# A gated mix of linear attention and an S-shifted MLP: the last 64 rows of W4 done in row tiles, and a re-ordered start

## The chip, the cores and the metric

The kernel runs on one core of one Trainium2 chip. The metric is the device time of one execution in microseconds (us); lower is better. Four runs of the kernel before took 267.59, 267.78, 267.78 and 268.14 us, the median is 267.78 us. The profile is of one further execution.

## The reference

With x of 2048 rows and 640 features, in bfloat16, the output is `g*a + (1-g)*b`, row by row:

```
g = sigmoid((x * gate_w).sum(-1))
a = linear attention of x (32 heads of 20 features, phi(q), phi(k), weights wqkv 640x1920, then wo 640x640)
h  = gelu(layernorm(x) @ w1)                       # 640 x 640
hs = (four quarters of h, shifted by +1, -1, +2, -2 rows) @ w2
x1 = x + hs
b  = x1 + gelu(layernorm(x1) @ w3) @ w4            # w3 640 x 1728, w4 1728 x 640
```

The change touches two places: the first products of the kernel, `k = x @ wk` together with the gate's dot product, and the last product, `... @ w4`, whose contraction runs over 1728 features. 1728 is 13 blocks of 128 and a rest of 64.

## The kernel before

Work is in blocks of 128 rows (16 of them, `c`), and in the MLP in tiles of 512 rows (`TS`, 4 of them, `t`), each of 4 blocks (`cc`). Every engine runs its instructions in the order in which the program writes them; nothing is rescheduled. All products go into PSUM tiles from one pool, `pair()`, of which there are four: each holds two banks of 128 x 512 float32, and a product of 640 output features is done as two halves (`hf`) of 320, one in each bank. A fifth `pair()` waits until the first is free.

**The start.** The SP queue (L124, L118, L130) and the ACT queue issue the loads: block 0 of x first, the five 128-row blocks of the k weights (`wk_sb`, one `load_wk` each; 0, 2, 4 on ACT and 1, 3 on SP), the gate vector `g5` (5 x 128) on SP, and then seven DMA transposes that bring the other blocks of x into `xT`. TensorE begins with six 512-wide products of constants (`warmup`, L202) that nobody reads, then transposes block 0 of x (L210), VectorE copies the transpose to `xT` (L211), and after two 128-wide products of constants the k products of block 0 follow (`k_mm`, L190), in the order 0, 2, 1, 4, 3 of the weight blocks and with the gate vector's transpose (L215) and its copy into column 640 of `wk_sb` (L216) in between. Blocks 1 to 15 then follow, each with ten k products of 320 or 321 columns; ScalarE and VectorE take each result out of PSUM (`k_evac`).

**The middle.** Then come q (L231), the sums over rows for the attention (L306), w1 (L340), the attention's small products (L359, L246, L378, L258), and w2 (L416). Of these, L246 and L378 use the array in narrow column tiles (the profile's form 128*32), L258 in row tiles (32*128).

**The MLP's tiles.** For each `t`, the w3 products (L463, 13 feature blocks of 128, results gelu'd by ScalarE at L471 into `h2`) alternate with the w2 products of the next tile and the attention's last product of this one (L447). The rest of 64 features of w3 (L468) is done in two column tiles (128*64), 256 rows of the tile each, so that in `h2` partitions 0 to 63 hold the 64 features for rows 0 to 255 and partitions 64 to 127 hold the same features for rows 256 to 511.

Then `w4_unit` runs for the four blocks of the tile. For each half it does 14 products of 320 columns (L488): 13 over full blocks and one over the rest. For the rest, `w4_sb` holds W4's last 64 rows twice, once in partitions 0 to 63 and once in 64 to 127, in two 128-row slots whose other half is set to zero by GpSimd (L395, L396). The product over all 128 partitions thus adds zeros for the rows of the other block. VectorE combines the result with the gate and with x1 (L494), SP stores it (L497). In the very last block each half has a `pair()` of its own and is taken out (L490) and stored (L492) by itself. `x1_scale` (L440), on ScalarE, scales the next tile's x1 by `1-g`.

Of the kernel before, what the change touches and what calls it, by code (L numbers as in the profile page):

```python
# [8 lines left out]
ALU = mybir.AluOpType  # L9
BF16 = mybir.dt.bfloat16  # L10
# [6 lines left out]
def kernel(  # L17
# [13 lines left out]
    nc = tc.nc  # L31
    P = 128
    S, D = A_x.shape[1], A_x.shape[2]
    F = B_w3.shape[1]
    H, Dh = 32, 20
    NCH = S // P
    TS = 512
    NT = S // TS
    CPT = TS // P
    DC = D // P  # L40
    HD = D // 2
    FF = F // P
    FR = F - FF * P
# [12 lines left out]
    out2 = out.rearrange("b s d -> (b s) d")  # L56
# [8 lines left out]
    outp = ctx.enter_context(tc.tile_pool(name="outp", bufs=2))  # L65
# [3 lines left out]
    def pair():  # L69
        return ps.tile([P, 2, 512], F32, name="pp")  # L70
# [15 lines left out]
    ident = const.tile([P, P], BF16)  # L86
    g5 = const.tile([DC, P], BF16)
# [8 lines left out]
    omg = const.tile([P, NCH], F32)  # L96
# [10 lines left out]
    wk_sb = st1.tile([P, DC, D + 16], BF16)  # L107
# [7 lines left out]
    sp, aq, gq = nc.sync, nc.scalar, nc.gpsimd  # L115

    def load_x(c0, c1):
        sp.dma_start(x_sb[:, c0:c1, 0:D], x2[c0 * P:c1 * P, :].rearrange("(c p) d -> p c d", p=P))  # L118
# [4 lines left out]
    def load_wk(q, dc):  # L123
        q.dma_start(wk_sb[:, dc, 0:D], A_wqkv[dc * P:(dc + 1) * P, D:2 * D])  # L124

    load_x(0, 1)
    load_wk(aq, 0)
    load_wk(aq, 2)
    load_wk(sp, 1)
    sp.dma_start(g5[:], gate_w.rearrange("(c p) -> c p", p=P))  # L130
    load_wk(aq, 4)
    load_wk(sp, 3)
    for c0, c1 in ((1, 2), (2, 3), (3, 4), (4, 6), (6, 8), (8, 12), (12, 16)):
        load_xT(c0, c1)
    sp.dma_start(wq_sb, wqkv_v[:, :, 0:D])
# [50 lines left out]
    def k_mm(pt, c, dcs, hfs=(0, 1), last=DC - 1):  # L186
        for dc in dcs:
            for hf in hfs:
                n = HD + hf
                nc.tensor.matmul(pt[:, hf, 0:n], lhsT=xT[:, dc, c * P:(c + 1) * P],  # L190
                                 rhs=wk_sb[:, dc, hf * HD:hf * HD + n], start=(dc == 0), stop=(dc == last))

    def k_evac(pt, c):
        nc.scalar.copy(ylog[:, c:c + 1], pt[:, 1, HD:HD + 1])
        phi(pk[:, c, :].rearrange("p (h e) -> p h e", h=2), pt[:, :, 0:HD], D)
# [4 lines left out]
    def warmup(n, w=TS):  # L200
        for i in range(n):
            nc.tensor.matmul(warm[:, 1, 0:w], lhsT=one[:, 0:P], rhs=one[:, 0:w], start=True, stop=True)  # L202

    warmup(6)
    kp = pair()
    turns = [(pair()[:, 0, :].bitcast(BF16), a, b) for a, b in ((0, 2), (2, DC))]
    tg = warm[:, 0, :].bitcast(BF16)
    for n, (ptb, a, b) in enumerate(turns):
        for dc in range(a, b):
            nc.tensor.transpose(ptb[:, (dc - a) * P:(dc - a + 1) * P], x_sb[:, 0, dc * P:(dc + 1) * P], ident[:])  # L210
        nc.vector.tensor_copy(xT[:, a:b, 0:P], ptb[:, 0:(b - a) * P].rearrange("p (c s) -> p c s", c=b - a))  # L211
    warmup(2, P)
    order = (0, 2, 1, 4, 3)
    k_mm(kp, 0, order[:3], (0,), order[4])
    nc.tensor.transpose(tg[:, 0:DC], g5[:], ident[0:DC, 0:DC])  # L215
    nc.vector.tensor_copy(wk_sb[:, :, D], tg[:, 0:DC])  # L216
    k_mm(kp, 0, order[3:4], (0,), order[4])
    k_mm(kp, 0, order[:4], (1,), order[4])
    k_mm(kp, 0, order[4:], last=order[4])
    k_evac(kp, 0)  # L220
    for c in range(1, NCH):
        pt = pair()
# [168 lines left out]
        ln1_apply(3 * CPT + cc)  # L391
    s1.close()
    w4p = ctx.enter_context(tc.tile_pool(name="w4p", bufs=1))
    w4_sb = w4p.tile([P, FF + 2, D], BF16)
    nc.gpsimd.memset(w4_sb[FR:P, FF, :], 0.0)  # L395
    nc.gpsimd.memset(w4_sb[0:FR, FF + 1, :], 0.0)  # L396
    nc.gpsimd.dma_start(w4_sb[:, 0:FF, :], B_w4[0:FF * P, :].rearrange("(c p) f -> p c f", p=P))
    nc.gpsimd.dma_start(w4_sb[0:FR, FF, :], B_w4[FF * P:F, :])
    nc.gpsimd.dma_start(w4_sb[FR:P, FF + 1, :], B_w4[FF * P:F, :])
    h2p = ctx.enter_context(tc.tile_pool(name="h2p", bufs=1))  # L400
    x1p = ctx.enter_context(tc.tile_pool(name="x1p", bufs=8))
    st = {}
# [6 lines left out]
    def w2_unit(t, cc):  # L409
        c = t * CPT + cc  # L410
        if cc == 0:
            st[t] = dict(x1=[], mv=small.tile([P, CPT, 2], F32, name="mv2"))
        pt = pair()
        for hf in range(2):
            for fc in range(DC):
                nc.tensor.matmul(pt[:, hf, 0:HD], lhsT=hsT[:, fc, 2 + c * P:2 + (c + 1) * P],  # L416
                                 rhs=w2_sb[:, fc, hf * HD:(hf + 1) * HD], start=(fc == 0), stop=(fc == DC - 1))
        x1 = x1p.tile([P, D], F32, name="x1")
        nc.vector.tensor_tensor(x1[:].rearrange("p (h e) -> p h e", h=2), pt[:, :, 0:HD],  # L419
                                x_sb[:, c, 0:D].rearrange("p (h e) -> p h e", h=2), op=ALU.add)  # L420
        ln_stats(st[t]["mv"][:, cc, :], x1[:], small.tile([P, 2, 6], F32, name="bnst")[:])
        st[t]["x1"].append(x1)

    def ln2_rstd(t, c0, c1):
        if c0 == 0:
            st[t]["rstd"] = small.tile([P, CPT], F32, name="rstd2")
        rsqrt(st[t]["rstd"][:, c0:c1], st[t]["mv"][:, c0:c1, 1])
# [9 lines left out]
    def x1_scale(t, cc):  # L437
        c = t * CPT + cc
        x1 = st[t]["x1"][cc]
        nc.scalar.activation(x1[:], x1[:], ACT.Copy, scale=omg[:, c:c + 1])  # L440
# [13 lines left out]
    def w3_unit(t, i):  # L454
        if "h2" not in st[t]:
            st[t]["h2"] = h2p.tile([P, FF * TS + LT], BF16, name="h2")
        h2, lnT = st[t]["h2"], st[t]["lnT"]
        pt = pair()
        for k in range(2):
            fc = 2 * i + k  # L460
            if fc < FF:
                for dc in range(DC):
                    nc.tensor.matmul(pt[:, k, :], lhsT=w3_sb[:, dc, fc * P:(fc + 1) * P], rhs=lnT[:, dc, :],  # L463
                                     start=(dc == 0), stop=(dc == DC - 1))
            else:
                for dc in range(DC):
                    for v in range(2):
                        nc.tensor.matmul(pt[FR * v:FR * (v + 1), k, 0:LT], lhsT=w3_sb[:, dc, FF * P:F],  # L468
                                         rhs=lnT[:, dc, v * LT:(v + 1) * LT], start=(dc == 0), stop=(dc == DC - 1))
        n = 2 * TS if 2 * i + 1 < FF else TS + LT  # L470
        nc.scalar.activation(h2[:, 2 * i * TS:2 * i * TS + n], pt[:].rearrange("p h e -> p (h e)")[:, 0:n],  # L471
                             ACT.Gelu_apprx_tanh)

    def w4_unit(t, cc):
        c = t * CPT + cc
        h2, x1 = st[t]["h2"], st[t]["x1"][cc]
        last = c == NCH - 1
        oc = outp.tile([P, D], BF16, name="oc")
        pts = [pair(), pair()] if last else [pair()] * 2
        for hf in range(2):  # L480
            hs = slice(hf * HD, (hf + 1) * HD)
            for fc in range(FF + 1):
                if fc < FF:
                    w, l = w4_sb[:, fc, hs], h2[:, fc * TS + cc * P:fc * TS + (cc + 1) * P]
                else:
                    v, o = cc // 2, FF * TS + (cc % 2) * P
                    w, l = w4_sb[:, FF + v, hs], h2[:, o:o + P]
                nc.tensor.matmul(pts[hf][:, hf, 0:HD], lhsT=l, rhs=w, start=(fc == 0), stop=(fc == FF))  # L488
            if last:
                nc.vector.scalar_tensor_tensor(oc[:, hs], pts[hf][:, hf, 0:HD], omg[:, c:c + 1], x1[:, hs],  # L490
                                               op0=ALU.mult, op1=ALU.add)
                nc.sync.dma_start(out2[c * P:(c + 1) * P, hs], oc[:, hs])  # L492
        if not last:
            nc.vector.scalar_tensor_tensor(oc[:].rearrange("p (h e) -> p h e", h=2), pts[0][:, :, 0:HD],  # L494
                                           omg[:, c:c + 1], x1[:].rearrange("p (h e) -> p h e", h=2),
                                           op0=ALU.mult, op1=ALU.add)
            nc.sync.dma_start(out2[c * P:(c + 1) * P, :], oc[:])  # L497

    for cc in range(CPT):
        w2_unit(0, cc)  # L500
# [16 lines left out]
    for t in range(NT):  # L517
        for i in range(NW3):
            w3_unit(t, i)
            if i < CPT and t + 1 < NT:  # L520
                w2_unit(t + 1, i)
            if 2 <= i < 2 + CPT:
                att_unit(t, i - 2)
        if t + 1 < NT:
            ln2_rstd(t + 1, 0, CPT)
            for cc in range(CPT):
                ln2_apply(t + 1, cc)
        for cc in range(CPT):
            if t + 1 < NT:
                x1_scale(t + 1, cc)  # L530
            w4_unit(t, cc)


# [28 lines left out]
```

## Time and profile before

| | |
|---|---|
| median of four runs | 267.78 us (267.59 to 268.14) |
| the profiled execution | 267.77 us |
| its span, first to last instruction | 266.1 us |
| around the span | 1.67 us |
| TensorE busy | 260.1 us, 98% of the span |
| VectorE, ScalarE, GpSimd busy | 140.3, 84.3, 24.1 us |
| DMA moved | 23.62 MB |
| chain of waits that ended last | 95% on TensorE |

Times in the profile are counted from the start of the span. A row of a group gives line, engine, operation, the tile written and those read, the form (rows*columns of the array that are used, then partitions x elements), the count, the busy time and the mean of one in ns, and behind the second bar the engine's idle time just before. "PEld" is TensorE's weight load, which has rows of its own. The durations of products overlap, since they are pipelined: what one product costs in a stream is the distance of its start from the next one's start.

### The profile page before, as it was taken

The page shows a single profiled execution, that of the slowest core. Times are in us where ns is not written, and L with a number is a line of the kernel's source. Part 1 is how long each engine was busy: PE and PEld are TensorE (multiplying, and loading weights), DVE is VectorE, ACT ScalarE, POOL GpSimd, SP SyncE. Part 2 cuts the span into 40 slices and gives each one's busy share as a digit, 9 for nine tenths or more (in the row PEclk, how much of TensorE's full clock was granted, in tenths as well). Part 3 has the DMA queues.
Part 4 walks back from the last instruction along what each step waited for, and adds up shares of the span by engine and source line. Part 5 has one row for each costly group of instructions (what it writes and reads, how often), then busy time and mean ns, then how long its engine had stood idle before and what let it go on. Part 6 is the DMA issues. An engine that isn't in the chain of part 4 may idle for free.

```text
span 266.1 us, 4240 instructions
## 1 busy us (share of the span) xinstructions
PE 260.1 (98%) x1720; PEld 163.4 (61%) x1736; DVE 140.3 (53%) x270; ACT 84.3 (32%) x122; POOL 24.1 (9%) x60
## 2 busy tenths in 40 slices
PE   7999999999999999999999999999999999999994
PEld 3677555788755644565676556577556577455673
DVE  1688688899857788945422364521464512122122
ACT  1555544321165646531510312420212340333100
POOL 7100010012323140001000001000001000000000
PEclk9999999999999999999999999999999999999999
DMA  7999977025668942000231000141000051000011
GB/s 191 174 240 365 378 229 291 0 46 122 129 96 252 201 76 52 0 0 0 46 84 48 25 0 2 25 99 52 25 0 2 1 123 52 25 0 2 0 49 49
DMA packets 44749, 23.62 MB, mean 89 GB/s; under 512 B 35450, under 2 KB 43642, under 8 KB 44730
## 3 DMA queue, kind: packets, MB, share of 16 engines
q1 hardware_dynamic: 43802, 20.57, 30.7%
q0 software_dynamic: 496, 2.29, 2.6%
q10 hardware_dynamic: 432, 0.49, 0.6%
q8 instruction: 13, 0.21, 0.3%
q14 instruction: 6, 0.05, 0.1%
HBM read 12.21 MB, written 2.62 MB: 56 GB/s over the span
## 4 chain that ended last, share of the span: by engine, by line
PE 95%; DMA 2%; ACT 1%; issue 0%; ACTq 0%; DVE 0%
PE pp L488 23%; PE pp L463 21%; PE pp L306 8%; PE pp L416 8%; PE pp L447 8%; PE pp L190 8%; PE pp L340 8%; PE pp L231 8%; DMA wk_sb<-in_A_wqkv_dram 2%; PE pp L468 1%; ACT m_sb L380 1%; PE pp L359 1%; PE pp L246 0%; ACTq L124 0%; PE pp L378 0%
## 5 line engine op out<-in xcount | busy, mean ns | idle before, releaser
L488 PE MATMUL pp<-w_sb,h 128*128 128x320 bf16 x448 | 61.5, 299 | 0.0
L471 ACT ACTIVATE h<-pp 128x1024 bf16<-128x1024 f32 (+1 forms) x28 | 27.8, 993 | 103.8 <-PE pp L463 95.4
L463 PE MATMUL pp<-lnxT,w_sb 128*128 128x512 bf16 x249 | 59.8, 379 | 0.6
L488 PEld LDWEIGHTS <-h 128*128 128x128 bf16 x448 | 43.5, 98 | 17.5 <-issue 0.8
L463 PEld LDWEIGHTS <-w_sb 128*128 128x128 bf16 x260 | 25.4, 98 | 26.7
L494 DVE SCALAR_TENSOR_TENSOR oc<-pp,omg,x 128x640 bf16<-128x640 f32 x15 | 13.3, 884 | 44.7 <-PE pp L488 44.7
L450 DVE SCALAR_TENSOR_TENSOR x<-pp,gate,x 128x640 f32<-128x640 f32 x16 | 13.9, 868 | 29.4 <-PE pp L447 29.4
L182 ACT ACTIVATE e<-pp 128x640 bf16<-128x640 f32 (+1 forms) x26 | 21.5, 827 | 9.6 <-PE pp L231 9.6
L447 PE MATMUL pp<-m_sb,pqT 128*128 128x320 bf16 x160 | 24.3, 299 | 0.0
L419 DVE TENSOR_TENSOR x<-pp,x_sb 128x640 f32<-128x640 f32 x16 | 13.1, 820 | 21.0 <-PE pp L416 21.0
L416 PE MATMUL pp<-w_sb,hsT 128*128 128x320 bf16 x160 | 23.9, 299 | 0.1
L190 PE MATMUL pp<-wk_sb,xT 128*128 128x320 bf16 (+1 forms) x160 | 22.5, 300 | 0.3 <-DMA wk_sb<-in_A_wqkv_dram 0.3
L306 PE MATMUL pp<-x_sb,pk 128*128 128x320 bf16 (+1 forms) x160 | 22.3, 300 | 0.0
L231 PE MATMUL pp<-xT,hsT 128*128 128x512 bf16 x98 | 21.6, 379 | 0.1
L306 PEld LDWEIGHTS <-pk 128*128 128x128 bf16 x160 | 18.8, 117 | 3.5
L416 PEld LDWEIGHTS <-hsT 128*128 128x128 bf16 x160 | 15.6, 98 | 8.2 <-issue 0.2
L447 PEld LDWEIGHTS <-pqT 128*128 128x128 bf16 x160 | 15.7, 98 | 7.7
L190 PEld LDWEIGHTS <-xT 128*128 128x128 bf16 x160 | 15.5, 98 | 6.9 <-issue 0.3
L340 PE MATMUL pp<-lnxT,w_sb 128*128 128x512 bf16 x77 | 17.8, 379 | 0.2
L231 PEld LDWEIGHTS <-hsT 128*128 128x128 bf16 x100 | 11.8, 118 | 9.7
L276 POOL TENSOR_SCALAR rstd<-mv 128x4 f32<-128x4 f32 (+1 forms) x11 | 3.4, 312 | 148.2 <-DVE mv L282 148.2
L184 DVE SCALAR_TENSOR_TENSOR pk<-pp,e 128x640 bf16<-128x640 f32 x16 | 13.2, 825 | 1.7
(79 smaller groups left out, 187.7 us busy)
## 6 DMA issues: line engine op xcount, KB each, us to landing
out_dram<-oc SPq DMA_DIRECT2D x15, 160.0 KB, 1.8
w_sb<-in_B_w_dram SPq DMA_DIRECT2D x1, 2160.0 KB, 9.2
w_sb<-in_B_w_dram POOLq DMA_DIRECT2D x1, 2080.0 KB, 10.6
x_sb<-in_A_x_dram SPq DMA_DIRECT2D x2, 640.0 KB, 10.0
x_sb<-in_A_x_dram SPq DMA_DIRECT2D x1, 1120.0 KB, 8.2
wo_sb<-in_A_wo_dram SPq DMA_DIRECT2D x6, 160.0 KB, 7.3
hsT<-in_A_wqkv_dram SPq DMA_DIRECT2D x1, 800.0 KB, 5.6
m_sb<-in_A_wqkv_dram SPq DMA_DIRECT2D x1, 800.0 KB, 11.0
```

The costliest lines, as they stand in the source:

```text
L182: nc.scalar.activation(ev, src, ACT.Exp)
L190: nc.tensor.matmul(pt[:, hf, 0:n], lhsT=xT[:, dc, c * P:(c + 1) * P], rhs=wk_sb[:, dc, hf * HD:hf * HD + n], start=(dc == 0), stop=(dc == ...
L231: nc.tensor.matmul(pt[:, t % 2, :], lhsT=wq_sb[:, dc, :].rearrange("p (m j) -> p j m", j=DC)[:, j], rhs=xT[:, dc, t * TS:(t + 1) * TS], st ...
L306: nc.tensor.matmul(pt[:, hf, 0:HD + hf], lhsT=w, rhs=x_sb[:, c, hf * HD:(hf + 1) * HD + hf], start=(c == 0), stop=(c == NCH - 1))
L340: nc.tensor.matmul(pt[:, i, :], lhsT=w, rhs=lnxT[t][:, dc, :], start=(dc == 0), stop=(dc == DC - 1))
L416: nc.tensor.matmul(pt[:, hf, 0:HD], lhsT=hsT[:, fc, 2 + c * P:2 + (c + 1) * P], rhs=w2_sb[:, fc, hf * HD:(hf + 1) * HD], start=(fc == 0), ...
L447: nc.tensor.matmul(pt[:, hf, 0:HD], lhsT=pqT[:, j, c * P:(c + 1) * P], rhs=m_sb[:, j, hf * HD:(hf + 1) * HD], start=(j == 0), stop=(j == D ...
L450: nc.vector.scalar_tensor_tensor(x1, pt[:, :, 0:HD], gate[:, c:c + 1], x1, op0=ALU.mult, op1=ALU.add)
L463: nc.tensor.matmul(pt[:, k, :], lhsT=w3_sb[:, dc, fc * P:(fc + 1) * P], rhs=lnT[:, dc, :], start=(dc == 0), stop=(dc == DC - 1))
L471: nc.scalar.activation(h2[:, 2 * i * TS:2 * i * TS + n], pt[:].rearrange("p h e -> p (h e)")[:, 0:n], ACT.Gelu_apprx_tanh)
L488: nc.tensor.matmul(pts[hf][:, hf, 0:HD], lhsT=l, rhs=w, start=(fc == 0), stop=(fc == FF))
L494: nc.vector.scalar_tensor_tensor(oc[:].rearrange("p (h e) -> p h e", h=2), pts[0][:, :, 0:HD], omg[:, c:c + 1], x1[:].rearrange("p (h e) - ...
```

## The change

1. W4's rest. `w4_sb` has one slot for the rest instead of two, with W4's last 64 rows in both halves and no zeros; the two GpSimd memsets are gone. `w4_unit` is replaced by `w4_tile`: for blocks 0 and 2 the 13 full products of each half (`w4_mm`), then one block of eight products for all four blocks (`w4_rest`), each over 64 partitions only, alternating between partitions 0 to 63 (blocks 0 and 1) and 64 to 127 (blocks 2 and 3), then blocks 1 and 3. The rest's products end the sums of blocks 0 and 2 and begin those of blocks 1 and 3. All four `pair()` of the pool are held at once. In the last tile the order after the rest is first half of block 3, both halves of block 1, second half of block 3; the two halves of block 3 are taken out by themselves (`w4_part`).
2. The loads. The gate vector is the first load on the ACT queue, ahead of wk blocks 0, 2 and 4; wk blocks 1 and 3 follow x on SP.
3. The first products. Three 128-wide products of constants follow the six wide ones; the gate vector is transposed between the two parts of the transpose of x; three 128-wide products of constants follow; then the k products of block 0 in the order 0 to 4, with one 256-wide product of constants between one weight block and the next.

```diff
     load_x(0, 1)
+    aq.dma_start(g5[:], gate_w.rearrange("(c p) -> c p", p=P))
+    load_wk(sp, 1)
     load_wk(aq, 0)
     load_wk(aq, 2)
-    load_wk(sp, 1)
-    sp.dma_start(g5[:], gate_w.rearrange("(c p) -> c p", p=P))
+    load_wk(sp, 3)
     load_wk(aq, 4)
-    load_wk(sp, 3)
...
     warmup(6)
+    warmup(3, P)
...
         nc.vector.tensor_copy(xT[:, a:b, 0:P], ptb[:, 0:(b - a) * P].rearrange("p (c s) -> p c s", c=b - a))
-    warmup(2, P)
-    order = (0, 2, 1, 4, 3)
-    k_mm(kp, 0, order[:3], (0,), order[4])
-    nc.tensor.transpose(tg[:, 0:DC], g5[:], ident[0:DC, 0:DC])
-    nc.vector.tensor_copy(wk_sb[:, :, D], tg[:, 0:DC])
-    k_mm(kp, 0, order[3:4], (0,), order[4])
-    k_mm(kp, 0, order[:4], (1,), order[4])
-    k_mm(kp, 0, order[4:], last=order[4])
+        if n == 0:
+            nc.tensor.transpose(tg[:, 0:DC], g5[:], ident[0:DC, 0:DC])
+            nc.vector.tensor_copy(wk_sb[:, :, D], tg[:, 0:DC])
+    warmup(3, P)
+    for dc in range(DC):
+        k_mm(kp, 0, (dc,))
+        if dc < DC - 1:
+            warmup(1, 2 * P)
...
-    w4_sb = w4p.tile([P, FF + 2, D], BF16)
-    nc.gpsimd.memset(w4_sb[FR:P, FF, :], 0.0)
-    nc.gpsimd.memset(w4_sb[0:FR, FF + 1, :], 0.0)
+    w4_sb = w4p.tile([P, FF + 1, D], BF16)
...
-    nc.gpsimd.dma_start(w4_sb[FR:P, FF + 1, :], B_w4[FF * P:F, :])
+    nc.gpsimd.dma_start(w4_sb[FR:P, FF, :], B_w4[FF * P:F, :])
...
-    def w4_unit(t, cc):
...
+    def w4_mm(t, cc, pts, hf, start):
+        dst, a, b = w4_dst(cc, pts, hf)
+        for fc in range(FF):
+            nc.tensor.matmul(dst, lhsT=st[t]["h2"][:, fc * TS + cc * P:fc * TS + (cc + 1) * P],
+                             rhs=w4_sb[:, fc, a:b], start=start and fc == 0, stop=not start and fc == FF - 1)
+
+    def w4_rest(t, pts):
+        for u in range(2):
+            for hf in range(2):
+                for v in range(2):
+                    rows = slice(FR * v, FR * (v + 1))
+                    dst, a, b = w4_dst(u + 2 * v, pts, hf)
+                    nc.tensor.matmul(dst, lhsT=st[t]["h2"][rows, FF * TS + u * P:FF * TS + (u + 1) * P],
+                                     rhs=w4_sb[rows, FF, a:b], start=u == 1, stop=u == 0)
...
+    def w4_tile(t):
+        pts = {cc: pair() for cc in (0, 2)}
+        for cc in (0, 2):
+            if t + 1 < NT:
+                x1_scale(t + 1, cc)
+            for hf in range(2):
+                w4_mm(t, cc, pts, hf, True)
+        for cc in (1, 3):
+            pts[cc] = pair()
+        w4_rest(t, pts)
+        for cc in (0, 2):
+            w4_out(t, cc, pts[cc])
+        last = t == NT - 1
+        for cc, hf in ((3, 0), (1, 0), (1, 1), (3, 1)) if last else ((1, 0), (1, 1), (3, 0), (3, 1)):
+            if t + 1 < NT and hf == 0:
+                x1_scale(t + 1, cc)
+            w4_mm(t, cc, pts, hf, False)
+            if last and cc == 3:
+                w4_part(t, cc, pts, hf)
+            elif hf == 1:
+                w4_out(t, cc, pts[cc])
```

`w4_out` combines and stores a whole block as before (one 640-wide operation, one store), `w4_part` does so for one half.

More of the change, by code (lines that the diff above doesn't have):

```diff
@@ L472, in w3_unit, with w4_dst @@
                              ACT.Gelu_apprx_tanh)
-    def w4_unit(t, cc):
+    def w4_dst(cc, pts, hf):
+        return pts[cc][:, hf, 0:HD], hf * HD, (hf + 1) * HD
+    def w4_mm(t, cc, pts, hf, start):
[11 more added lines that the diff above has]
+                                     rhs=w4_sb[rows, FF, a:b], start=u == 1, stop=u == 0)
@@ L475, in w4_unit, with w4_out @@
+    def w4_out(t, cc, pt):
         c = t * CPT + cc
-        h2, x1 = st[t]["h2"], st[t]["x1"][cc]
-        last = c == NCH - 1
+        x1 = st[t]["x1"][cc]
         oc = outp.tile([P, D], BF16, name="oc")
[L479 to L497, printed above, removed]
+        nc.vector.scalar_tensor_tensor(oc[:].rearrange("p (h e) -> p h e", h=2), pt[:, :, 0:HD],
+                                       omg[:, c:c + 1], x1[:].rearrange("p (h e) -> p h e", h=2),
+                                       op0=ALU.mult, op1=ALU.add)
@@ new lines, in w4_out, with w4_part @@
+        nc.sync.dma_start(out2[c * P:(c + 1) * P, :], oc[:])
+    def w4_part(t, cc, pts, hf):
+        c = t * CPT + cc
+        src, a, b = w4_dst(cc, pts, hf)
+        oc = outp.tile([P, D], BF16, name="oc")
+        nc.vector.scalar_tensor_tensor(oc[:, a:b], src, omg[:, c:c + 1], st[t]["x1"][cc][:, a:b],
+                                       op0=ALU.mult, op1=ALU.add)
+        nc.sync.dma_start(out2[c * P:(c + 1) * P, a:b], oc[:, a:b])
+    def w4_tile(t):
[19 more added lines that the diff above has]
+                w4_out(t, cc, pts[cc])
@@ L527 @@
                 ln2_apply(t + 1, cc)
[L528 to L531, printed above, removed]
+        w4_tile(t)
 _INS = ['A_x', 'A_wqkv', 'A_wo', 'B_x', 'B_w1', 'B_w2', 'B_w3', 'B_w4', 'gate_w']
```

## The prediction

> **What bounds the kernel now.** I read the page first: busy times, the chain's summary, the groups of the changed line.
>
> ```profile
> PE 260.1 (98%) x1720; PEld 163.4 (61%) x1736; DVE 140.3 (53%) x270; ACT 84.3 (32%) x122; POOL 24.1 (9%) x60
> ...
> PE 95%; DMA 2%; ACT 1%; issue 0%; ACTq 0%; DVE 0%
> ...
> L488 PE MATMUL pp<-w_sb,h 128*128 128x320 bf16 x448 | 61.5, 299 | 0.0
> ...
> L488 PEld LDWEIGHTS <-h 128*128 128x128 bf16 x448 | 43.5, 98 | 17.5 <-issue 0.8
> ```
>
> TensorE is busy for 98% of the span and is 95% of the chain. Before the W4 products (L488) it idles 0.0 us. So a product saved there is saved in the time, until something else is late. The chain in order of time gives the prices:
>
> ```profile
> 128.36 1.08 PE pp L463 x5
> 129.44 0.67 PE pp L468 x10
> 130.10 15.32 PE pp L488 x112
> ...
> 148.94 2.16 PE pp L463 x10
> 151.10 1.36 PE pp L416 x10
> ```
>
> Ten products of 320 columns take 1.36 us, so one costs 0.136; one of 512 costs 0.216 (2.16/10). A tile's W4 stage is 112 products, 112 x 0.136 = 15.23 us; eight are the rest. And the column-tiled rest of w3 (L468), ten of 256 columns, takes 0.67 us: one after the other they would need 10 x 0.108 = 1.08, five overlapping pairs 0.54. They do run in pairs, and about 0.13 us is something else. The timeline in narrow windows shows what:
>
> ```profile
> 84.53 0.38 PE L340 MATMUL pp<-lnxT,w1x 128*128 128x512 bf16 x1
> 84.84 0.31 PE L378 MATMUL pp<-wo_sb,kvT 128*32 128x320 bf16 x2
> ...
> 87.44 0.31 PE L378 MATMUL pp<-wo_sb,kvT 128*32 128x320 bf16 x4
> 87.68 0.40 PE L258 MATMUL pp<-r_bf,emat 32*128 32x512 bf16 x4
> ...
> 88.00 0.39 PEld L416 LDWEIGHTS <-hsT 128*128 128x128 bf16 x3 [0.23 <-issue]
> ...
> 129.06 0.38 PE L463 MATMUL pp<-lnxT,w_sb 128*128 128x512 bf16 x1
> 129.37 0.30 PE L468 MATMUL pp<-lnxT,w_sb 128*64 128x256 bf16 x2
> ...
> 129.83 0.28 PE L468 MATMUL pp<-lnxT,w_sb 128*64 128x256 bf16 x2
> 130.03 0.31 PE L488 MATMUL pp<-w_sb,h 128*128 128x320 bf16 x1
> ```
>
> The first number is the start. From the last full product at 129.06 to the first narrow one at 129.37 pass 0.31 us, though a 512-wide one costs 0.216: entering costs 0.09. Leaving is 129.83 to 130.03, 0.20 against 0.108: 0.09 again. At 84.53 to 84.84 it is 0.09, from column to row tiles (87.44 to 87.68) 0.24 - 0.136 = 0.10. L258 is the one row-tiled place: four products of 512 columns lie within 0.40 us, where one alone shows 0.38, and the next weight load starts 0.32 after them, 0.216 + 0.10. So four row tiles run in the time of one, and the way back costs 0.10.
>
> At the start the timeline shows what releases what:
>
> ```profile
> 0.83 2.72 PE L202 MATMUL pp<-const-bfloat16-1.0 128*128 128x512 bf16 x6 [0.83 <-PEq L546]
> ...
> 3.98 0.71 PE L210 MATMUL pp<-ident,x_sb 128*128 128x128 bf16 x5 [0.42 <-POOL emat L162]
> ...
> 4.41 0.68 DVE L211 COPY xT<-pp 128x256 bf16<-128x256 bf16 x2 [4.41 <-PE pp L210]
> ...
> 5.52 0.17 PE L215 MATMUL pp<-ident,g 5*128 5x5 bf16 x1
> ...
> 6.01 14.16 PE L190 MATMUL pp<-wk_sb,xT 128*128 128x320 bf16 x102 [0.32 <-DMA wk_sb<-in_A_wqkv_dram]
> ...
> 7.06 12.92 PEld L190 LDWEIGHTS <-xT 128*128 128x128 bf16 x96 [0.27 <-DMA xT<-in_A_x_dram]
> ```
>
> TensorE waits for wk until 6.01, then has seven k products of block 0 left, to 6.96 (7 x 0.136), and block 1 begins at 7.06, when the first DMA transpose lands. From there L190 runs without a gap.
>
> **The change, part 1: W4's rest.** Per tile it removes 8 products of 0.136 us (1.09 us) and adds four pairs of row tiles. By L258 and L468 a pair costs one product, 0.136, so 0.54. It adds one entry into row tiles and one exit, 0.09 to 0.10 each by the rows above, and the first product after each switch is some 0.01 to 0.03 late (the first L468 pair took 0.13 of 0.67 - 0.54), so 0.22 for both. Net -1.09 + 0.54 + 0.22 = -0.33 us a tile, about -1.3 for four. From below: if the switches cost nothing, -0.54 a tile, -2.2; nothing in the rows suggests it. From above: if pairs do not overlap, 8 x 0.136 + 0.22 against 1.09, +0.22 a tile, +0.9.
>
> A rule speaks against this. In L488 a weight load takes 98 ns and is never seen between products: they start 0.136 apart, each with its own load into the same rows of the array. The Trainium skill (TensorE: Matmul & The Clock Gate, Part 3, the mechanism) says that a weight load overlaps products in flight only when it goes to another row group. In the new block a pair fills both row groups, so by that rule the next pair's loads are exposed: 4 x (0.136 + 0.098) + 0.22 = 1.16 a tile against 1.09, +0.07, or +0.3 us in all, no gain. By the rows, the load of the same row group is hidden: 448 times in L488, and with tiles in L468, where two loads a pair did not stretch the 0.108 spacing. I take the rows.
>
> What hides the rest of this part: VectorE now gets two 640-wide combinations (0.884 us each by L494) back to back after the rest, 1.8 us, while TensorE has 52 products, 7.1 us, before the tile's end; nobody waits for them but the stores and, four `pair()` later, the next tile. The next tile's first w3 product needs the `pair()` of block 0, taken out 5 us earlier; the last one, of block 3, is out 1.2 us after the tile's end and is wanted after w3, w2 and w3, 2.16 + 1.36 + 2.16 = 5.7 us. Without that cover, one 0.884 a tile would show. The gelu of the rest (L471, 0.99 us) now has 7 us until it is read; its other block is still wanted 12 products after the start, as before. `x1_scale` for blocks 1 and 2 change places on ScalarE, which has 3.7 us of work in a 15 us stage. The two memsets leave GpSimd's queue, so the W4 loads behind them are issued some 1.3 us earlier, at about 78; they are used at 130. After the last product the tail is as before: one half of 320 columns, one store; the store before it now carries a whole block, issued some 1.4 us earlier, and lands in 1.8 by the DMA rows, so about 0.4 after the last issue. Taken as nothing.
>
> **Part 2: the loads.** On ACT's queue the gate vector (one issue, about 0.38 us) goes ahead of wk 0, 2, 4 and of the table load, all 0.4 later; ScalarE's first work is at 7.17, the table load would end at 3.9. On SP's queue it is gone, so wk 3, the seven transposes and every later load are issued about 0.4 earlier. The bytes before the first transpose are the same and the DMA is full there (390 GB/s between 3 and 4 us), so its landing moves by -0.4 to 0.
>
> **Part 3: the first products.** The six wide constants start 0.42 us apart, so they and three more end at 3.7; x still comes at 3.97. Two transposes (0.11 apart), then the gate's (with a switch for its five rows, 0.10 each way), then three: to about 4.7. Then a new wait: the order of instructions shows the next product of constants waiting for VectorE, because the gate's transpose lies in the same tile as the constants' result. VectorE copies x's first part from 4.41 to 4.70, then the gate (0.18) to 4.9; TensorE goes on at 4.95. All of block 0 is behind that wait. Three constants to 5.2, then ten k products and four 256-wide constants, 10 x 0.136 + 4 x 0.109 = 1.80: 7.03. The weights are no longer waited for, but the constants are executed in order and fill what was won. Block 1 begins at 7.03 or when the transpose lands: -0.03 to +0.02 against 7.06. Bounds: -0.4 (everything 0.4 earlier, the constants cheaper) to +0.4 (gate vector late, wk 4 late on ACT). I take 0.
>
> **Sum.** -1.3 + 0 on the profiled execution: its span 266.1 becomes 264.8, with the 1.67 around it 266.5. Its own 267.77 is the median of the runs, 267.78, so it stands.
>
> **The rivals.**
> *The rule is right, or pairs overlap in part*: +0.3 us, 268.1. For: the trace has row tiles only once, with no second pair behind the first. Against: L468 and L488. 0.06.
> *Row tiles run one after the other (the slower side)*: in `w4_rest`, eight products at 0.136 and two switches, +0.9, 268.7. It decides from the pair's price: even at 0.217 us, slower by 0.2% above 0.25. Against: L258. 0.07.
> *The clock*: the wide constants start 0.42 apart, those of L463 0.216: TensorE starts at half speed and is at full speed by 6.01 (the clock row of the page, all nines, does not show it). The skill (same page, Part 1) says that full speed comes after a busy window of about 3.4 us that runs free of the kernel. With the new wait from 4.7 to 4.95 it could come a window later; by that rule 3.4 us at half speed, estimated at 1.6 us lost, so -1.3 + 1.6, 268.1. By the trace, TensorE is about as busy up to 5 us as before. 0.05.
> *The start gains too, or a switch is cheaper*: -0.3 to -0.7 more, 265.8 to 266.2. 0.09.
>
> **How the numbers follow.** The forecast has 0.73. About 0.2%, 0.54 us, is what a measurement of this kernel can tell from no change. Forecast and better start are faster: 0.82. The rule's case and the clock's are near 268.1, mostly within: 0.10. The serial case is slower, with a little of the others: 0.08. The forecast's own range is 266.0 to 267.0; the range reaches to the better start and some way to the partly overlapped pairs: 265.8 to 267.4.
>
> **What would show it.** Right: the eight rest products in pairs within 3 or 4 ns, pairs 0.136 apart, 0.09 to 0.10 at each end, a W4 stage of about 14.9 us from first product to the next w3; block 1 of k near 7.0. Wrong: loads visible between pairs, pairs 0.2 or more apart, idle time before w3 or w4 products with VectorE as releaser, or k products of block 0 that start 0.27 apart.

## The result, and the profile after

The changed kernel takes 266.79 us (median of 29 runs, 266.2 to 268.09) against 267.78 us before; the ratio is 0.9958, 95% interval 0.9945 to 0.9971, so 0.8 to 1.5 us less. The forecast was 266.5 us, faster, in a range of 265.8 to 267.4. The profiled execution took 266.79 us with a span of 265.1 us, 1.0 us below the 266.1 before. Lines have moved: w3 is L462, its rest L467, the full W4 products L479, the rest of W4 L488, the rows' sums of the attention L307.

The page after, busy times, chain and groups of W4:

```profile
PE 259.9 (98%) x1728; PEld 162.7 (61%) x1744; DVE 139.6 (53%) x270; ACT 84.3 (32%) x122; POOL 22.8 (9%) x58
...
PE 97%; ACT 1%; issue 0%; DVE 0%
...
L479 PE MATMUL pp<-w_sb,h 128*128 128x320 bf16 x416 | 57.9, 299 | 0.0
L479 PEld LDWEIGHTS <-h 128*128 128x128 bf16 x416 | 40.1, 98 | 17.0 <-issue 1.9
```

TensorE still sets the time, and still idles 0.0 us before W4's full products. In the chain's rows, `pp` is the PSUM tile written, L479 is W4's full products and L488 the rest. The chain in order of time (start, duration, what), first and last tile:

```profile
128.73 1.08 PE pp L462 x5
129.81 0.67 PE pp L467 x10
130.47 7.17 PE pp L479 x52
137.64 0.65 PE pp L488 x8
138.29 7.17 PE pp L479 x52
145.46 0.22 PE pp L462
...
246.70 7.17 PE pp L479 x52
253.87 0.65 PE pp L488 x8
254.51 7.18 PE pp L479 x52
261.70 0.03 issue
261.72 0.55 DVE oc L504
```

A tile's W4 stage is 130.47 to 145.46, 14.99 us, against 15.32 before (130.10 to 145.42): -0.33 a tile, four times -1.3. The timeline in narrow windows shows the block itself:

```profile
137.34 0.30 PE L479 MATMUL pp<-w_sb,h 128*128 128x320 bf16 x1
137.58 0.31 PE L488 MATMUL pp<-w_sb,h 64*128 64x320 bf16 x2
137.72 0.57 PE L488 MATMUL pp<-w_sb,h 64*128 64x320 bf16 x6
138.00 0.30 PE L488 MATMUL pp<-w_sb,h 64*128 64x320 bf16 x2
138.23 0.31 PE L479 MATMUL pp<-w_sb,h 128*128 128x320 bf16 x1
```

In is 137.34 to 137.58, 0.24 - 0.136 = 0.10; out is 138.00 to 138.23, 0.23 - 0.136 = 0.09. In between are three steps from pair to pair, 137.58 to 138.00, of 0.14 each. But the whole gained 1.0, not 1.3. The rest is at the start:

```profile
3.67 0.42 PE L211 MATMUL pp<-ident,x_sb 128*128 128x128 bf16 x2
...
4.83 0.74 PE L190 MATMUL pp<-wk_sb,xT 128*128 128x320 bf16 x2
5.36 0.42 PE L202 MATMUL pp<-const-bfloat16-1.0 128*128 128x256 bf16 x1
5.58 0.74 PE L190 MATMUL pp<-wk_sb,xT 128*128 128x320 bf16 x2
...
6.33 0.52 PE L190 MATMUL pp<-wk_sb,xT 128*128 128x320 bf16 x2
...
6.79 0.44 PE L190 MATMUL pp<-wk_sb,xT 128*128 128x320 bf16 x2
...
7.17 1.12 PE L190 MATMUL pp<-wk_sb,xT 128*128 128x320 bf16 x7
```

The k products of block 0 come as pairs, with a product of constants after each. From pair to pair it takes 4.83 to 5.58 = 0.75, then 0.75, 0.46, 0.38. The last is the full-speed price, two k products of 0.136 and one product of constants of 0.109; the first two are at half speed. Block 1 begins after the last pair, 7.17 + 0.27 = 7.44, against 7.06 before. That +0.38 stays to the attention's sums, which begin at 49.63 instead of 49.26. Sum: -1.3 + 0.4, and the way from the last product to the end is 3.40 instead of 3.45: -1.0. These are two profiles, one run each; the experiments below show how much the start differs from run to run.

### The profile page after: what moved, and what is told of

Same layout as the page of the kernel before. It is cut to its first block, busy times and chain, and to the rows that moved or that the text cites. A ratio compares the mean times of both kernels' runs of the same rounds, so it can differ in the third digit from the quotient of the medians.

```text
span 265.1 us, 4251 instructions
## 1 busy us (share of the span) xinstructions
PE 259.9 (98%) x1728; PEld 162.7 (61%) x1744; DVE 139.6 (53%) x270; ACT 84.3 (32%) x122; POOL 22.8 (9%) x58
## 4 chain that ended last, share of the span: by engine, by line
PE 97%; ACT 1%; issue 0%; DVE 0%
PE pp L479 22%; PE pp L462 21%; PE pp L190 8%; PE pp L307 8%; PE pp L415 8%; PE pp L446 8%; PE pp L341 8%; PE pp L232 8%; PE pp L202 2%; PE pp L467 1%; PE pp L488 1%; ACT m_sb L381 1%; PE pp L360 1%; PE pp L247 0%; PE pp L379 0%
## 5 line engine op out<-in xcount | busy, mean ns | idle before, releaser
L462 PE MATMUL pp<-lnxT,w_sb 128*128 128x512 bf16 x249 | 59.8, 379 | 0.6
L479 PE MATMUL pp<-w_sb,h 128*128 128x320 bf16 x416 | 57.9, 299 | 0.0
L479 PEld LDWEIGHTS <-h 128*128 128x128 bf16 x416 | 40.1, 98 | 17.0 <-issue 1.9
L462 PEld LDWEIGHTS <-w_sb 128*128 128x128 bf16 x260 | 25.5, 98 | 26.7
L190 PE MATMUL pp<-wk_sb,xT 128*128 128x320 bf16 (+1 forms) x160 | 23.2, 304 | 0.0
L307 PE MATMUL pp<-x_sb,pk 128*128 128x320 bf16 (+1 forms) x160 | 22.3, 300 | 0.0
L307 PEld LDWEIGHTS <-pk 128*128 128x128 bf16 x160 | 18.8, 117 | 3.5
L183 DVE TENSOR_SCALAR e<-e 128x640 bf16<-128x640 bf16 (+1 forms) x26 | 9.6, 369 | 8.8 <-ACT e L182 7.2
```

The source lines that it names most:

```text
L307: nc.tensor.matmul(pt[:, hf, 0:HD + hf], lhsT=w, rhs=x_sb[:, c, hf * HD:(hf + 1) * HD + hf], start=(c == 0), stop=(c == NCH - 1))
L479: nc.tensor.matmul(dst, lhsT=st[t]["h2"][:, fc * TS + cc * P:fc * TS + (cc + 1) * P], rhs=w4_sb[:, fc, a:b], start=start and fc == 0, stop ...
```

## The experiments

**The two parts apart: e1 and e2.** e1 is the changed kernel with the old loads and first products, e2 the kernel before with the new ones.

```diff
# e1_w4only: in the changed kernel
-    aq.dma_start(g5[:], ...)  ahead of wk 0; warmup(3, P); warmup(1, 2 * P) between the weight blocks
+    loads and first products as before
# e2_startonly: in the kernel before
+    loads and first products as in the change; w4_unit kept
```

> W4's part of the change alone, on the old loads and first products. If the gain is all in W4's rest and the start gives some of it back: W4 stage 14.99 us a tile as in the changed kernel against 15.32 before, 4 x 0.33 = 1.3 us less than before, so about 266.5 us and below the changed kernel. Rival, the start also gains: this one is slower than the changed kernel, above 266.8. Rival, the four-pair hold of PSUM or the double evacuation costs something outside the stage: gain under 1.1 us.

> The new loads and first products alone, with the old W4. If the start costs what the changed kernel's profile shows (block 1 of k begins at 7.44 instead of 7.06): +0.2 to +0.4 us over before on the typical run, with a wider spread from run to run than before, since products in order at half speed are no longer hidden by a wait. Rival, the start is neutral or gains: 267.3 to 267.8.

W4 alone took 266.45 us (ratio 0.9948, 0.9930 to 0.9966), what the forecast gave for both parts. The start alone took 268.15 against 267.81 for the runs before beside it: +0.34 by the medians, but the ratio, 1.0007 (0.9993 to 1.0020), does not exclude zero. The profiles tell more. "Full speed" is the moment from which the trace's record of the granted clock reads 1.0; the distances between the starts of products halve there. "Again" is a second profile (e9 to e11); e3 and e4, described below, have the change's start. All in us:

| | full speed | block 1 of k begins | attention's sums begin |
|---|---|---|---|
| before | 5.0 | 7.06 | 49.26 |
| W4 alone, again | 5.6, 3.9 | 6.87, 6.79 | 49.13, 49.24 |
| the change, again | 6.5, 6.3 | 7.44, 7.34 | 49.63, 49.52 |
| start alone | 6.4 | 7.40 | 49.59 |
| e4 | 6.7 | 7.56 | 49.75 |
| e3 | 5.6 | 7.00 | 50.06 |
| no constants between the weight blocks, again | 6.1, 6.8 | 6.89, 7.25 | 49.09, 49.43 |

(e3 and W4 alone's second profile wait again, later, for transposes of x.) With the new start, block 1 begins the later, the later full speed comes; e3's timeline has the first pair alone at half speed:

```profile
4.83 0.74 PE L190 MATMUL pp<-wk_sb,xT 128*128 128x320 bf16 x2
...
5.58 0.44 PE L190 MATMUL pp<-wk_sb,xT 128*128 128x320 bf16 x2
...
6.72 1.53 PE L190 MATMUL pp<-wk_sb,xT 128*128 128x320 bf16 x10
```

Block 1 begins there at 7.00, earlier than before. So the +0.38 between the two profiles above belongs to the start and to the moment of full speed together: at nearly the same moment, e3 reaches block 1 0.13 after W4 alone. Whether the new start itself makes full speed later, or the profiled runs happened to fall so, is not shown.

**What the gain is: e3 and e6.** e3 keeps the eight products of a block and changes their order, e6 puts all eight on partitions 0 to 63 (blocks 2 and 3 then get the rest of blocks 0 and 1).

```diff
# e3_v_outer
-        for u in range(2):
-            for hf in range(2):
-                for v in range(2):
+        for v in range(2):
+            for u in range(2):
+                for hf in range(2):
# e6_one_group
-                    rows = slice(FR * v, FR * (v + 1))
+                    rows = slice(0, FR)
```

> The changed kernel with the loop over the two partition halves moved outside in w4_rest: the same eight products, but four of one half and then four of the other. If the gain is the overlap of the two halves: seven steps of 0.136 instead of four, block 0.65 + 3 x 0.136 = 1.06 us, +0.41 a tile, +1.6 us in all (268.4), all of the gain gone. Rival, the order does not matter since the hardware takes products of the other half ahead: no change. Rival, weight loads into the same row group are exposed: steps of 0.23, +0.98 a tile, +3.9 us.

> The changed kernel with all eight products of w4_rest on partitions 0 to 63 (blocks 2 and 3 get the rest of blocks 0 and 1 instead of their own). Same count of products, one row group. If the gain is the overlap of two row groups: steps of 0.136 us one after the other, block 8 x 0.136 + 0.22 = 1.3 us instead of 0.65, +0.65 a tile, +2.2 to +2.6 in all. If loads into the same row group were exposed: steps of 0.23, block about 2.1.

The chain of e3 and then of e6 in the first tile:

```profile
130.90 7.17 PE pp L479 x52
138.07 0.66 PE pp L488 x8
138.73 7.17 PE pp L479 x52
```

```profile
130.95 7.17 PE pp L479 x52
138.12 1.19 PE pp L488 x8
139.31 7.17 PE pp L479 x52
```

e6 is nearly as expected: 1.19 us, where 0.65 was: +0.54 a tile (said: +0.65), and 269.43 us in its one run. Four tiles make 2.2 of the 2.6 us over the change; the rest lies, in the profile, before W4, where TensorE waits for a transpose of x near 16.7 us. Eight products in one row group cost the old price each, 8 x 0.136 and one switch of 0.10, so half the products' time was saved by two row groups at once, not by shorter products over 64 partitions. Weight loads for the same row group stayed hidden; exposed, at 98 ns each, they would have made it about 2 (an estimate).

e3 went against my expectation: 0.66 us and 266.70 us. The program gives four products to one half and then four to the other, and they still ran in pairs. In the trace the second product that starts waits for the semaphore that, in the changed kernel, the first product of the upper half waits for; in e3's program that product is the fifth. So here a product of a free row group started ahead of earlier ones of the busy group, and the alternation that `w4_rest` writes out is not what makes the pairs. That every engine runs in the order of the program does not hold for these products. Within a pair the starts lie 13 to 15 ns apart, against 3 or 4 in the change. What makes the pairs was not tested further.

**What a switch costs: e4.**

```diff
# e4_two_blocks: in w4_tile
             for hf in range(2):
                 w4_mm(t, cc, pts, hf, True)
+            if cc == 0:
+                pts[1], pts[3] = pair(), pair()
+                w4_rest(t, pts, (1,))
-        w4_rest(t, pts)
+        w4_rest(t, pts, (0,))
```

> The changed kernel with w4_rest in two blocks of two pairs: the starting sums of blocks 1 and 3 after block 0, the ending ones of blocks 0 and 2 after block 2. One more entry and exit a tile. If a switch pair costs 0.21 us as the rows before gave: +0.21 a tile, +0.85 us, 267.65. Rival, part of the cost is the one drain already paid or is hidden: under +0.4 us.

```profile
130.59 3.64 PE pp L479 x26
134.23 0.38 PE pp L488 x4
134.61 3.64 PE pp L479 x26
138.24 0.38 PE pp L488 x4
138.62 7.17 PE pp L479 x52
```

The next w3 product begins at 145.79, so the stage is 145.79 - 130.59 = 15.20 us, 0.21 more than with one block, as the rows before gave; the whole took 267.51 us, 0.72 above the change where four times 0.21 is 0.84 (ratio to before 0.9982, 0.9966 to 0.9998). The overlap is worth 0.54 a tile; one way in and out leaves 0.33 of it, two leave 0.12. That the rest of all four blocks is done in one block is what keeps most of the gain.

**What the start loses: e7 and e5.** e7 puts 20 wide products of constants ahead instead of 6, so that everything is loaded; e5 leaves out the four between the weight blocks.

```diff
# e7_long_warm
-    warmup(6)
+    warmup(20)
# e5_no_fill
         k_mm(kp, 0, (dc,))
-        if dc < DC - 1:
-            warmup(1, 2 * P)
```

> The changed kernel with 20 wide products of constants at the start instead of 6, so that all loads are in and TensorE is at full speed when block 0 comes. If the clock alone made the start slower than forecast: from the first k product of block 0 to the first of block 1 it takes 10 x 0.136 + 4 x 0.109 = 1.80 us as forecast, instead of 2.6. Rival, a wait inside (weights, gate column, PSUM): longer than 1.9.

> The changed kernel without the four 256-wide products of constants between the k products of block 0. If what the start loses is half-speed work executed in order, block 1 of k begins about 4 x 0.11 to 4 x 0.21 us earlier than the changed kernel's for the same moment of full speed, and not before the first transpose at 6.63: 6.65 to 7.0, and the whole 266.0 to 266.4, as good as W4 alone (266.45) or better. Rival, the constants are needed to bring full speed: without them it comes one window later more often, and the median is above the changed kernel's 266.79.

Timeline of e7, block 0:

```profile
8.13 0.43 PE L190 MATMUL pp<-wk_sb,xT 128*128 128x320 bf16 x2
...
8.51 0.44 PE L190 MATMUL pp<-wk_sb,xT 128*128 128x320 bf16 x2
...
8.89 0.44 PE L190 MATMUL pp<-wk_sb,xT 128*128 128x320 bf16 x2
...
9.66 0.71 PE L190 MATMUL pp<-wk_sb,xT 128*128 128x320 bf16 x4
```

All steps are 0.38, and block 1 begins 1.80 us after the first k product, the forecast's figure. No wait is in the block; what the changed kernel has more, 0.37 + 0.37 + 0.08, is half speed. In e5 block 0 ends early enough to wait for the first transpose (weight loads with their wait):

```profile
6.89 1.20 PEld L190 LDWEIGHTS <-xT 128*128 128x128 bf16 x10 [0.25 <-DMA xT<-in_A_x_dram]
```

It took 266.54 us (0.9962, 0.9950 to 0.9973), about the time of W4 alone. So the rival that the constants are needed there for full speed did not come about.

**What the constants are good for: e8 and e12.** e8 has W4's part and the new loads, but the old first products (in the order 0 to 4). e12 adds three 256-wide products of constants before the first and three before the third k product.

```diff
# e8_loads: in the changed kernel
-    first products of the change
+    first products as before, with order = (0, 1, 2, 3, 4)
# e12_loads_fill: in e8_loads
     warmup(2, P)
+    warmup(3, 2 * P)
...
+    k_mm(kp, 0, order[:2], (0,), order[4])
+    warmup(3, 2 * P)
+    k_mm(kp, 0, order[2:3], (0,), order[4])
```

> W4's part and the new order of loads, with the old first products but in the order 0 to 4 of the weight blocks. If the earlier issue of the loads is worth something by itself: x's block 0 lands near 3.1 and the first transpose near 6.63, block 1 of k begins 0.1 to 0.3 earlier than in W4 alone (6.87 to 7.06), about 266.3. Rival, block 0 is bound by half-speed products, not by loads: same as W4 alone, 266.4 to 266.5.

> The kernel with the new loads and the old first products (e8_loads), with three 256-wide products of constants before the first k product and three before the third, where TensorE sat idle for 0.57 and 0.68 us. If those gaps delayed full speed by a window: its runs near 268 (half of them in e8_loads) become one in four or fewer, and the median falls from 267.4 to 266.4 to 266.8. Rival, the late full speed has another cause, such as the moment of the start: still about half near 268.

e8's median, 267.37, lies between two groups: seven of 14 runs took 266.32 to 266.64 us, seven 268.09 to 269.12 (ratio 0.9975, 0.9947 to 1.0002). The profile is of the second kind:

```profile
4.66 0.69 PE L190 MATMUL pp<-wk_sb,xT 128*128 128x320 bf16 x2 [0.36 <-DMA wk_sb<-in_A_wqkv_dram]
5.83 0.42 PE L190 MATMUL pp<-wk_sb,xT 128*128 128x320 bf16 x1 [0.47 <-DMA wk_sb<-in_A_wqkv_dram]
6.19 0.18 PE L215 MATMUL pp<-ident,g 5*128 5x5 bf16 x1
...
6.64 3.06 PE L190 MATMUL pp<-wk_sb,xT 128*128 128x321 bf16 x11
...
9.27 0.98 PE L190 MATMUL pp<-wk_sb,xT 128*128 128x320 bf16 x5
```

x came early and then TensorE stood still for the weights, twice. The products from 6.64 to 9.27 are ten steps in 2.63 us, 0.26 each: half speed up to 9.5 us. With constants put there (e12) one of 16 runs is above 268 and the median is 266.99. That speaks for the gaps putting off full speed, and against the rival that would have left half of the runs there; but the two sets ran on two chips, and of the long runs only e8's was profiled. The median is not 266.4 to 266.8 as I expected: in e12's profile the third k product comes only at 6.40, after 0.76 us for a late weight block, and block 0 lasts the longer.

**The three once more, on one chip.**

> The changed kernel once more, beside W4 alone and the version without constants between the weight blocks, on one chip. Expected 266.6 to 266.9 and the highest of these three, if its start loses a few tenths to W4 alone.

> W4's part alone once more: 266.3 to 266.5, 0.2 to 0.4 below the changed kernel. Rival, the start is neutral: within 0.1 of it.

> The changed kernel without the constants between the weight blocks once more: 266.3 to 266.6. If the loads moved earlier are worth what the profile shows, level with W4 alone or a little below.

The change 266.86 us (0.9945, 0.9924 to 0.9966), W4 alone 266.55 (0.9952, 0.9936 to 0.9969), without constants in between 266.56 (0.9936, 0.9912 to 0.9959). The medians repeat the 0.3; the ratios overlap wholly. The spans of the single runs show two effects in these times.

First, each kernel with the old start has a group of long spans: 33 of 130 runs of the kernel before at 267.4 us or more, the others at 266.7 or less; W4 alone has ten of 39 at 266.0 or more. The start alone has none of 22 above 266.7, the change three of 37 at 266.0 or more. I take these groups for the late full speed of e8; no run of them was profiled. The typical span is longer with the new start: the median is 265.1 for the change, 264.8 for W4 alone.

Second, in the four kernels with constants between the weight blocks that were run often (the change, start alone, e3, e4), 37 of 90 runs took over 1.8 us outside the span, up to 3.15. In the kernels without them (before, W4 alone, e5, e8) none of 206 did, in e12 one of 16. Why is open. There is one lead: e4's profiled run took 268.62 us with a span of 266.1, and its trace has one more load of instructions, 16 KB at 267.84, after the last instruction. e7, with 14 more products, has that load within the span, at 261.16. The other traces don't have it, e3's among them, with 1.97 us outside.

The means over both sets are 266.89 for W4 alone and 266.96 for the change. So the new start lengthens the usual run and seems to make the long ones rarer; on the mean it is worth nothing that these runs show.

## Why the prediction was right

*The W4 sum* was right in each term within 0.03: a pair 0.14 (said: 0.136), in 0.10 and out 0.09 (0.22 for both, with 0.03 for late first products), -0.33 a tile (-0.33). W4 alone gave the forecast's 266.5 us. The choice of the rows over the Trainium skill's rule on weight loads held: e6 has eight loads into one row group, one after the other, at the old product's price. (The same section, Part 3, the mechanism, also lets a load into "the background weight buffer" go ahead; the prediction took only half of it.) The serial rival is what e6 shows for one row group, and did not come about with two.

*The cover* held: no idle time appears before W4. Before w3 the rows show 0.6 us in both profiles, each with only 249 of 260 products on record; in e3, with all 260, it is 0.0. The tail is 3.40 against 3.45.

*The start* was taken as 0 and was +0.38 in the profile. The step that failed is "ten k products and four 256-wide constants, 10 x 0.136 + 4 x 0.109 = 1.80". The work was right, as e7 shows; its price was not: I took the full-speed price for everything after 5 us, because the kernel before was at full speed by 6.01. In that profile it came at 5.0, in the changed kernel's only near 6.5, so the term was 2.6, not 1.8. A second error hid part of it, which was luck. I kept x at 3.97; it came at 3.67 or before, since TensorE no longer waited for it, and all of block 0 began 0.4 earlier, at 4.83 instead of 5.2. At full speed that would have given 4.83 + 1.80 = 6.63 at best, a gain of 0.4.

*The clock rival* named the cause, but as all or nothing, a whole window at 0.05. In the traces the moment moves from run to run, from 5.6 to 6.7 us with the very same start (e3, e4). By the skill's account (TensorE: Matmul & The Clock Gate, Part 1) the window runs free of the kernel, which fits; no run here shows the window itself. Before, waits for weights covered part of such work; the change replaces the waits by work that costs double at half speed.

## What to carry to other kernels

Where a product's contraction has a rest of half the array, two such rests in two row groups run at once, and pay if enough of them stand together to bear about 0.2 us for going in and out. Products of constants that fill a wait may bring full speed in time more often (e12 against e8), but between products that are about to be ready they cost their own time, and twice that while the clock is still at half speed. Price the first microseconds of a kernel by the speed that its own rows show there, for an early and a late moment of full speed. Look at the spread of runs as well as the median, and at the time outside the span: one profile of each kernel can mistake the moment of full speed for the change.

## What the runs showed that I had not expected

Products of different row groups need not start in program order: in e3 a block written as four and four ran as four pairs, 0.66 us against 0.65. With gaps of half a microsecond on TensorE around 4 to 6 us, half of the runs took about 2 us longer (e8: medians of the two groups 266.50 and 268.48), and the one profiled had full speed only at 9.5 us. And with constants between the weight blocks, four runs in ten took up to 1.5 us more outside the span; the cause is open.
